# Two v loads on Sync's queue, two casts on Scalar, and block 1's turning one unit later

## The chip, the cores and the metric

The kernel runs on one core of a Trainium2 chip. A core has five engines with queues of their own: TensorE (PE in the profile; PEld is its weight load), VectorE (DVE), ScalarE (ACT), GpSimd (POOL) and SyncE (SP). Transfers are issued by SP, ACT or POOL and are moved by 16 DMA engines. The metric is the device time of one execution in microseconds. The profile is one execution; its times are counted from the start of its span.

## The reference, cut to what matters

Linear attention with a decay per head, followed by a gated feed-forward layer. There are 4 batches, 8 heads, 768 positions and a head size of 64; the layer has a width of 512 and a hidden width of 1536.

```python
for b in range(nb):                     # blocks of the sequence
    intra = einsum('bhic,bhjc->bhij', qb, kb) * Dmask[None]
    intra = einsum('bhij,bhjd->bhid', intra, vb)
    inter = einsum('bhid,bhde->bhie', qb * lam_pow[None], kv_state)
    out[:, :, sl] = intra + inter
    kv_state = lam_block * kv_state + einsum('bhsd,bhse->bhde', kb * rev_pow, vb)
x = out.transpose(0, 2, 1, 3).reshape(B * S, H * D)
gate = 1 / (1 + exp(-(x @ w_gate)))
return (gate * (x @ w_val)) @ w_out
```

All inputs and the output are fp32 in memory. Dmask is lam to the power of the distance, and zero above the diagonal.

## The kernel before

The sequence is cut into six blocks of 128 positions. A block holds 4 x 128 = 512 tokens, all batches together. Matmuls take bf16 and sum in fp32. For each block the kernel does three things. It computes the attention: q and k are transposed, multiplied (`sp`), multiplied by the decay mask (`MT`), multiplied by v (`op`), and the result is cast into `XT`, the transposed input of the layer. It computes 12 units of the hidden layer: for each 128 hidden columns a gate matmul with WG, a sigmoid (`sg`), a value matmul with WV, and a product (`ht`). And it multiplies the 12 `ht` tiles by WO for each batch (`po`), copies the result to `ob` and stores it. The state `Sb` is carried from block to block.

The order of work on each engine is the program's own order: the kernel is written with a manual schedule, in which each engine runs its instructions as the Python code issues them. Waits between engines are put in by the framework.

These parts touch the change:

- **The loads of block 0** (lines 112 to 152). q of batch 0 comes as fp32 into `q01[0]` over ACT's queue, q of batch 1 into `q01[1]` over SP's. VectorE casts the first (line 500) and ACT the second (line 165) into `Q[0]`. All other loads are issued by POOL, with a cast to bf16 on the way, in this order: k of batches 0 and 1, k of 2 and 3, q of 2, q of 3, v of 0, v of 1, v of 2, then the first 128 columns of WG, v of 3, the first 128 columns of WV, and the next 128 columns of each. WG and WV in chunks of 256 columns follow.
- **The small constants** (lines 154 to 173). ACT makes `lnl`, `pk`, `lnp`, `lamq0`, the cast of q of batch 1, `kds` and `dec`. `lamq0` scales the transposed q of block 0. The mask is made by VectorE from `tri` and `pk` in two halves (`make_mask`).
- **Attention of block 0** (lines 499 to 534). `piece_tq0` transposes and scales one batch's q. `piece_tk0` transposes two batches' k; its copies to `KS` are ACT's, but for one on VectorE. `piece_s` multiplies, `piece_m` masks, `piece_a0` multiplies by v and casts to `XT[0]`, on ACT but for the last half. ACT loads the table for the sigmoid (line 512) after the second pair's `KS` copies. `idle(n)` issues n matmuls on a tile of zeros, which feed nothing. The first hidden unit is written out in parts between the last steps.
- **Weights and block 1's inputs** (lines 536 to 543). POOL issues chunk 3 of WG and WV, makes `KD[0]`, then loads q and k of block 1's first two batches, chunk 4, chunk 5, and the rest of block 1. Chunk i holds hidden units 2i and 2i + 1.
- **The units of block 0, and the attention of block 1's first pair between them** (lines 565 to 590). `t(1, 0)` transposes q and k of block 1's first two batches on PE, `sc` multiplies and masks the first, `m` masks the second, and `a` multiplies by state and v and casts to `XT[1]`, two copies on ACT (line 340). They stand between units 7 and 11.
- **The stores** (line 493). SP issues them. For block 0 the tiles of batches 0 and 1 are stored in two halves of 64 rows.

Of the kernel before, what the change touches and what calls it, by code (L numbers as in the profile page):

```python
# [7 lines left out]
FP32 = mybir.dt.float32  # L8
BF16 = mybir.dt.bfloat16
AF = mybir.ActivationFunctionType  # L10
# [5 lines left out]
def kernel(  # L16
# [11 lines left out]
    nc = tc.nc  # L28

    B, H, S, D = q.shape  # L30
    C = 128
# [38 lines left out]
    def load(n, what, b0, b1):  # L70
        sl = slice(n * C, (n + 1) * C)
        for c in what:
            lst, src = {"q": (Q, q), "k": (K, k), "v": (V, v)}[c]
            if n > 1 and c != "v":
                lst[n] = qkv.tile([128, 2, B, HP, D], BF16, tag=c + "b", name=c + "b")
                for e in range(2):
                    nc.gpsimd.dma_start(  # L77
                        out=lst[n][:, e].rearrange("p b y d -> p (b y) d"),
                        in_=src[:, e::2, sl, :].rearrange("b y s d -> s (b y) d"))
                continue  # L80
            if n == 1 and c != "v":
                if n not in lst:
                    lst[n] = qkv.tile([128, 2, B * H * D // 2], BF16, tag=c + "b", name=c + "b")
                if b0 == 0:
                    nc.gpsimd.dma_start(
                        out=lst[n][:, 0].rearrange("p (x d) -> p x d", d=D),
                        in_=src[b0:b1, :, sl, :].rearrange("b h s d -> s (b h) d"))
                else:
                    for e in range(2):
                        nc.gpsimd.dma_start(  # L90
                            out=lst[n][:, 1].rearrange("p (e x d) -> p e x d", e=2, d=D)[:, e],
                            in_=src[b0:b1, e::2, sl, :].rearrange("b y s d -> s (b y) d"))
                continue
            if n not in lst:
                lst[n] = qkv.tile([128, B, H, D], BF16, tag=c + "b", name=c + "b")
            nc.gpsimd.dma_start(  # L96
                out=lst[n][:, b0:b1],
                in_=src[b0:b1, :, sl, :].rearrange("b h s d -> s (b h) d"))
# [5 lines left out]
    def load_gv(i, w):  # L104
        load_w(WG, wg_r, i, w)
        load_w(WV, wv_r, i, w)
# [5 lines left out]
    q01 = [const.tile([128, H, D], FP32, tag=f"q{b}f", name=f"q{b}f") for b in range(2)]  # L112
    nc.scalar.dma_start(out=q01[0], in_=q[0, :, 0:C, :].rearrange("h s d -> s h d"))
    nc.sync.dma_start(out=q01[1], in_=q[1, :, 0:C, :].rearrange("h s d -> s h d"))
    Q[0] = qkv.tile([128, B, H, D], BF16, tag="qb", name="qb")
    nc.scalar.preload_act_table_set("natural_log_exp_and_others")
    ident = const.tile([128, 128], BF16, tag="ident")
# [23 lines left out]
    load(0, "k", 2, 4)  # L141
    load(0, "q", 2, 3)
    load(0, "q", 3, 4)
    load(0, "v", 0, 1)
    load(0, "v", 1, 2)
    load(0, "v", 2, 3)
    GW = DFF // 6
    load_w(WG, wg_r, 0, GW // 2)
# [4 lines left out]

    lnl = const.tile([128, H], FP32, tag="lnl")
    nc.scalar.activation(lnl, lam_bc, AF.Ln)
    pk = const.tile([128, H], FP32, tag="pk")
    nc.scalar.activation(pk, lnl, AF.Exp, scale=jn[:, 0:1])
    lnp = const.tile([128, HP], FP32, tag="lnp")
    for u in range(2):
        us = slice(u * 64, (u + 1) * 64)  # L160
# [1 line left out]
    lamq0 = const.tile([128, HP, C], BF16, tag="lamq0")  # L162
    for hp in range(HP):
        nc.scalar.activation(lamq0[:, hp, :], ip1, AF.Exp, scale=lnp[:, hp:hp + 1])
    nc.scalar.copy(Q[0][:, 1], q01[1])
    kds = const.tile([128, H], FP32, tag="kds")
    nc.scalar.activation(kds, lnl, AF.Exp, scale=jn[:, 1:2])
# [22 lines left out]
    def make_mask(u):  # L190
        nc.vector.tensor_tensor(
            out=mask[:, u::2, :], in0=tri.unsqueeze(1).to_broadcast([128, HP, C]),
            in1=pk[:, u::2].unsqueeze(2).to_broadcast([128, HP, C]), op=ALU.mult)
# [21 lines left out]
    def idle(n):  # L215
        for i in range(n):
            nc.tensor.matmul(wm, lhsT=zero[:, :128], rhs=zero, start=True, stop=True,
                             skip_group_check=True)
# [33 lines left out]
    def piece_tq0(bs, then=None):  # L252
        tq = ps_at.tile([128, 2, 2, 2 * C], BF16, name="tq", tag="ps")
        for b in bs:
            if (0, b // 2) not in QS:
                QS[0, b // 2] = trsb.tile([128, 2, 2, 2, C], BF16, tag="QS", name="QS")
            for g in range(HP):
                transpose_pair(tq[:, b % 2, g // 2, g % 2 * C:g % 2 * C + C], Q[0], b, g)
        if then:
            then()  # L260
        for b in bs:
            nc.vector.tensor_tensor(out=QS[0, b // 2][:, :, b % 2].rearrange("p e x c -> p e (x c)"),
                                    in0=tq[:, b % 2], in1=lamq0_e, op=ALU.mult)

    def piece_tk0(bp):
        tk = ps_at.tile([128, 2, 2, 2 * C], BF16, name="tk", tag="ps")
        for i in range(2):
            for g in range(HP):
                transpose_pair(tk[:, i, g // 2, g % 2 * C:g % 2 * C + C], K[0], 2 * bp + i, g)
        KS[0, bp] = trsb.tile([128, 2, 2, 2, C], BF16, tag="KS", name="KS")  # L270
        for i in range(2):
            cp = nc.vector.tensor_copy if bp == 0 and i == 0 else nc.scalar.copy
            cp(KS[0, bp][:, :, i].rearrange("p e x c -> p e (x c)"), tk[:, i])
# [44 lines left out]
    def piece_a(n, pairs):  # L318
        OP = {(bp, u): ps_at.tile([128, 2, 2, C], FP32, name="op", tag="ps")
              for bp in pairs for u in range(2)}  # L320
        for bp in pairs:
            for i in range(2):
                for x in range(2):
                    for u in range(2):
                        for e in range(2):
                            nc.tensor.matmul(OP[bp, u][half(e), x, i, :],  # L326
                                             lhsT=Sb[half(u), 2 * bp + i, 2 * e + x, :],
                                             rhs=QS[n, bp][half(u), e, i, x, :],
                                             start=(i == 0 and x == 0), stop=False,
                                             skip_group_check=True)  # L330
        for bp in pairs:
            for u in range(2):
                for i in range(2):
                    for x in range(2):
                        intra(n, 2 * bp + i, OP[bp, u][:, x, i, :], 2 * x + u, False, i == 1 and x == 1)
        if n not in XT:
            XT[n] = xtp.tile([128, NMT, B, C], BF16, tag="XT", name="XT")
        for bp in pairs:
            for u in range(2):
                nc.scalar.copy(XT[n][:, u::2, 2 * bp:2 * bp + 2, :], OP[bp, u])  # L340

    def piece_a0(b, split=False):
        if 0 not in XT:
# [89 lines left out]
    def mm_part(ps, W, n, ft, lo, hi):  # L433
        x = XT[n].rearrange("p m b c -> p m (b c)")
        for mt in range(NMT):
            nc.tensor.matmul(ps[:, lo:hi], lhsT=W[:, mt, ft * 128:(ft + 1) * 128], rhs=x[:, mt, lo:hi],  # L436
                             start=(mt == 0), stop=(mt == NMT - 1))

    def psum():
        return ps_ff.tile([128, TCH], FP32, name="gp", tag="ff")  # L440

    def sigm(n, ft, gp):
        HT[n, ft] = htp.tile([128, TCH], BF16, tag="sg", name="sg", bufs=3)
        nc.scalar.activation(HT[n, ft], gp, AF.Sigmoid)
# [37 lines left out]
    def piece_po(n, tt):  # L482
        po = ps_ff.tile([128, DM], FP32, name="po", tag="ff")
        for ft in range(NFT):
            nc.tensor.matmul(po, lhsT=HT[n, ft][:, tt * 128:(tt + 1) * 128],  # L485
                             rhs=WO[:, ft, :], start=(ft == 0), stop=(ft == NFT - 1))
        ob = osb.tile([128, DM], FP32, tag="ob", name="ob")
        nc.scalar.copy(ob, po)  # L488
        parts = 2 if n == 0 and tt < 2 else 1
        rows = 128 // parts  # L490
        for i in range(parts):
            lo = tt * S + n * C + i * rows
            nc.sync.dma_start(out=out[lo:lo + rows, :], in_=ob[i * rows:(i + 1) * rows, :])


    load_gv(1, GW)
# [1 line left out]

    idle(10)
    nc.vector.tensor_copy(Q[0][:, 0], q01[0])  # L500
    piece_tq0([0], lambda: make_mask(0))
    make_mask(1)
    idle(1)
    piece_tq0([1])
    piece_tk0(0)
    idle(1)
    piece_s(0, [0])
    piece_m(0, 0)
# [26 lines left out]

    load_gv(3, GW)
    make_kd(0)
    load(1, "qk", 0, 2)
    load_gv(4, GW)
    load_gv(5, GW)  # L540
    load(1, "v", 0, 2)
    load(1, "qk", 2, 4)
# [1 line left out]
    def t(n, bp):  # L544
        piece_t(n, bp)
# [8 lines left out]
    def a(n, *pairs):  # L554
        piece_a(n, pairs)

    def gv(n, *fts):
        for ft in fts:
            piece_gv(n, ft)
# [20 lines left out]
    for i in range(3):  # L580
        load_wo(i, NFT // 3)
    gv(0, 5, 6, 7)
    t(1, 0)
    gv(0, 8)
    sc(1, 0)
    gv(0, 9)
    m(1, 0)
    gv(0, 10)
    a(1, 0)
    gv(0, 11)  # L590
    transpose_half()
    load(2, "qkv", 0, B)
    transpose_by_dma(2)
# [91 lines left out]
```

## Time and profile before

| | |
|---|---|
| time, median of 3 runs | 227.29 us (227.24 to 228.84) |
| profiled execution | 227.16 us, span 225.4 us |
| granted TensorE clock | 1.000 |
| PE busy | 218.3 us (97%) |
| DVE busy | 103.2 us (46%) |
| POOL busy | 80.9 us (36%) |
| ACT busy | 79.8 us (35%) |
| queue q0 (POOL's transfers) | 81232 packets, 13.90 MB |
| queue q1 (SP's transfers) | 23568 packets, 11.28 MB |

A row of a group or timeline gives the start, the time taken, the engine and line, the operation, output <- input, and in square brackets the idle time before it and what ended it. Rows of matmuls overlap at their ends by the pipeline's depth. A DMA's "landing" is the time from its issue to the semaphore that says it is complete. The share of a queue is the sum of its packets' times over the time of all 16 engines, so several queues, or one with several packets under way in an engine, can exceed 100%.

### The profile page before, as it was taken

The numbers are of one execution on the slowest core, as the hardware profiler recorded it, in microseconds if no ns is written. First come the engines' busy times: TensorE is split into PE (matmuls) and PEld (weight loads), VectorE is DVE, ScalarE is ACT, GpSimd is POOL, SyncE is SP. The second block draws the span as 40 slices with busy tenths as digits, with TensorE's granted clock in tenths as the row PEclk, the third lists the DMA queues.
The fourth block names the chain that finished last, engine by engine and source line by source line (L and its number), as shares of the span: only waits on it lengthen the run. The fifth ranks groups of instructions, "written<-read, shape, count | busy, mean of one in ns | idle before, by whom it ended". The sixth has DMA issues, their size and how long they took to land.

```text
span 225.4 us, 4297 instructions
## 1 busy us (share of the span) xinstructions
PE 218.3 (97%) x1766; PEld 114.4 (51%) x1766; DVE 103.2 (46%) x190; ACT 79.8 (35%) x150; POOL 80.9 (36%) x76
## 2 busy tenths in 40 slices
PE   7689999999999999999999999999999999999994
PEld 2443454888854455444545444446444445444443
DVE  7865737486431622435742345742334850333300
ACT  3664243434422225333215333225333224433221
POOL 8999967983691007940005950000000000000000
DMA  6999999999999992999021999321900012100022
GB/s 109 156 173 195 173 193 156 155 198 166 157 172 181 208 188 82 208 154 119 2 96 47 183 155 157 20 96 50 225 9 0 0 49 93 49 0 0 0 93 97
DMA packets 105860, 25.72 MB, mean 114 GB/s; under 512 B 95984, under 2 KB 102896, under 8 KB 105840
## 3 DMA queue, kind: packets, MB, share of 16 engines
q0 software_dynamic: 81232, 13.90, 80.8%
q1 hardware_dynamic: 23568, 11.28, 20.5%
q10 hardware_dynamic: 1040, 0.26, 0.5%
q8 instruction: 14, 0.23, 0.5%
q14 instruction: 6, 0.05, 0.1%
HBM read 28.32 MB, written 6.29 MB: 154 GB/s over the span
## 4 chain that ended last, share of the span: by engine, by line
PE 91%; POOL 4%; DMA 3%; issue 0%; DVE 0%; POOLq 0%
PE po L485 27%; PE vp L428 22%; PE gp L422 22%; PE gp L457 5%; PE vp L463 5%; DMA WV<-in_moe_w_val_dram 3%; PE sp L302 2%; PE op L314 2%; PE gp L436 2%; POOL vb L96 2%; PE op L326 1%; PE cp L406 1%; PE po L474 1%; POOL kb L96 1%; POOL qb L96 1%; POOL WG L102 1%
## 5 line engine op out<-in xcount | busy, mean ns | idle before, releaser
L431 DVE TENSOR_TENSOR ht<-sg,vp 128x512 bf16<-128x512 bf16 x57 | 39.2, 688 | 68.5 <-PE vp L428 68.5
L485 PE MATMUL po<-WO,ht 128*128 128x512 bf16 x276 | 61.9, 379 | 0.0
L428 PE MATMUL vp<-XT,WV 128*128 128x512 bf16 x228 | 58.5, 379 | 0.4 <-DMA WV<-in_moe_w_val_dram 0.4
L422 PE MATMUL gp<-XT,WG 128*128 128x512 bf16 x228 | 58.6, 379 | 0.0
L425 ACT ACTIVATE sg<-gp 128x512 bf16<-128x512 f32 x57 | 34.1, 598 | 62.3 <-PE gp L422 62.2
L485 PEld LDWEIGHTS <-ht 128*128 128x128 bf16 x276 | 26.3, 98 | 31.0
L428 PEld LDWEIGHTS <-WV 128*128 128x128 bf16 x228 | 22.2, 98 | 27.6 <-DMA WV<-in_moe_w_val_dram 0.9
L422 PEld LDWEIGHTS <-WG 128*128 128x128 bf16 x228 | 21.7, 98 | 25.7
L488 ACT COPY ob<-po 128x512 f32<-128x512 f32 x23 | 13.5, 587 | 52.2 <-PE po L485 50.4
L199 DVE TENSOR_TENSOR MT<-sp,mask 128x512 bf16<-128x512 f32 x40 | 25.2, 683 | 10.0 <-PE sp L302 10.0
L387 POOL TENSOR_TENSOR sd<-Sb,dec 128x512 f32<-128x512 bf16 x8 | 8.2, 1037 | 43.2 <-DVE Sb L413 43.2
L457 PE MATMUL gp<-XT,WG 128*128 128x256 bf16 x96 | 14.4, 273 | 0.0
L463 PE MATMUL vp<-XT,WV 128*128 128x256 bf16 x96 | 14.4, 273 | 0.0
L467 DVE TENSOR_TENSOR ht<-sg,vp 128x256 bf16<-128x256 bf16 x24 | 10.0, 420 | 8.6 <-PE vp L463 8.6
L460 ACT ACTIVATE sg<-gp 128x256 bf16<-128x256 f32 x24 | 9.2, 385 | 12.6 <-PE gp L457 11.5
L96 POOL DMA_DIRECT2D vb<-in_v_dram x10 | 12.8, 1280 | 1.0 <-DVE QS L248 0.8
L378 POOL TENSOR_TENSOR kd<-kb,kds 128x1024 bf16<-128x1024 bf16 x6 | 11.3, 1906 | 3.5 <-DMA kb<-in_k_dram 3.5
L413 DVE TENSOR_TENSOR Sb<-cp,sd 128x512 bf16<-128x512 f32 x8 | 5.2, 686 | 15.5 <-PE cp L406 15.5
L340 ACT CAST XT<-op 128x512 bf16<-128x512 f32 x20 | 10.4, 599 | 3.0 <-PE op L314 3.0
L457 PEld LDWEIGHTS <-WG 128*128 128x128 bf16 x96 | 9.2, 98 | 1.7 <-issue 0.4
L463 PEld LDWEIGHTS <-WV 128*128 128x128 bf16 x96 | 9.4, 98 | 1.1
L77 POOL DMA_DIRECT2D qb<-in_q_dram x8 | 9.4, 1181 | 0.0
(82 smaller groups left out, 148.7 us busy)
## 6 DMA issues: line engine op xcount, KB each, us to landing
out_dram<-ob SPq DMA_DIRECT2D x21, 256.0 KB, 2.1
kb<-in_k_dram POOLq DMA_DIRECT2D x11, 256.0 KB, 8.8
qb<-in_q_dram POOLq DMA_DIRECT2D x9, 256.0 KB, 8.0
vb<-in_v_dram POOLq DMA_DIRECT2D x4, 512.0 KB, 14.1
WO<-in_moe_w_out_dram POOLq DMA_DIRECT2D x3, 512.0 KB, 8.2
WG<-in_moe_w_gate_dram POOLq DMA_DIRECT2D x5, 256.0 KB, 8.6
WV<-in_moe_w_val_dram POOLq DMA_DIRECT2D x5, 256.0 KB, 9.2
qb<-in_q_dram POOLq DMA_DIRECT2D x4, 128.0 KB, 8.1
```

What stands on the lines that cost most here:

```text
L96: nc.gpsimd.dma_start(out=lst[n][:, b0:b1], in_=src[b0:b1, :, sl, :].rearrange("b h s d -> s (b h) d"))
L199: nc.vector.tensor_tensor(out=out.rearrange("p (e x) c -> p e x c", e=2), in0=x.rearrange("p (e x) c -> p e x c", e=2), in1=mask.rearrange ...
L340: nc.scalar.copy(XT[n][:, u::2, 2 * bp:2 * bp + 2, :], OP[bp, u])
L378: nc.gpsimd.tensor_tensor(out=KD[n][:, e], in0=K[n][:, e], in1=kds[:, e::2].unsqueeze(1).unsqueeze(3).to_broadcast([128, B, HP, D]), op=AL ...
L422: nc.tensor.matmul(gp, lhsT=WG[:, mt, fs], rhs=x[:, mt, :], start=(mt == 0), stop=(mt == NMT - 1))
L425: nc.scalar.activation(sg, gp, AF.Sigmoid)
L428: nc.tensor.matmul(vp, lhsT=WV[:, mt, fs], rhs=x[:, mt, :], start=(mt == 0), stop=(mt == NMT - 1))
L431: nc.vector.tensor_mul(HT[n, ft], sg, vp)
L457: nc.tensor.matmul(gp[:, cs], lhsT=WG[:, mt, fs], rhs=x[:, mt, cs], start=(mt == 0), stop=(mt == NMT - 1))
L463: nc.tensor.matmul(vp[:, cs], lhsT=WV[:, mt, fs], rhs=x[:, mt, cs], start=(mt == 0), stop=(mt == NMT - 1))
L485: nc.tensor.matmul(po, lhsT=HT[n, ft][:, tt * 128:(tt + 1) * 128], rhs=WO[:, ft, :], start=(ft == 0), stop=(ft == NFT - 1))
L488: nc.scalar.copy(ob, po)
```

## The change

Five edits in one.

- v of batches 0 and 1 of block 0 is no longer loaded by POOL. SP loads it as fp32 into `q01[0]` and `q01[1]` once the q in them has been cast, and ACT casts it into `V[0]`, behind its first `KS` copy of block 0.
- ACT makes `pk` after `lamq0`. VectorE makes the first half of the mask after the first scaled q, and the second after the first pair's `KS`.
- Chunk 4 of WG and WV, units 8 and 9, is loaded ahead of block 1's first q and k; `t(1, 0)` comes after unit 8, `sc` and `m` after unit 9.
- Unit 11 is written in two parts with `a(1, 0)` between gate and value. Of that call's two `XT` copies one is VectorE's.
- The first two output tiles are stored whole.

```diff
+    V[0] = qkv.tile([128, B, H, D], BF16, tag="vb", name="vb")
...
-    load(0, "v", 0, 1)
-    load(0, "v", 1, 2)
     load(0, "v", 2, 3)
...
-    pk = const.tile([128, H], FP32, tag="pk")
-    nc.scalar.activation(pk, lnl, AF.Exp, scale=jn[:, 0:1])
...
     for hp in range(HP):
         nc.scalar.activation(lamq0[:, hp, :], ip1, AF.Exp, scale=lnp[:, hp:hp + 1])
+    pk = const.tile([128, H], FP32, tag="pk")
+    nc.scalar.activation(pk, lnl, AF.Exp, scale=jn[:, 0:1])
     nc.scalar.copy(Q[0][:, 1], q01[1])
...
-                nc.scalar.copy(XT[n][:, u::2, 2 * bp:2 * bp + 2, :], OP[bp, u])
+                cp = nc.vector.tensor_copy if n == 1 and bp == 0 and u else nc.scalar.copy
+                cp(XT[n][:, u::2, 2 * bp:2 * bp + 2, :], OP[bp, u])
...
-        parts = 2 if n == 0 and tt < 2 else 1
-        rows = 128 // parts
-        for i in range(parts):
-            lo = tt * S + n * C + i * rows
-            nc.sync.dma_start(out=out[lo:lo + rows, :], in_=ob[i * rows:(i + 1) * rows, :])
+        nc.sync.dma_start(out=out[tt * S + n * C:tt * S + (n + 1) * C, :], in_=ob)
...
     nc.vector.tensor_copy(Q[0][:, 0], q01[0])
-    piece_tq0([0], lambda: make_mask(0))
-    make_mask(1)
+    for b in range(2):
+        nc.sync.dma_start(out=q01[b], in_=v[b, :, 0:C, :].rearrange("h s d -> s h d"))
+    piece_tq0([0])
+    make_mask(0)
     idle(1)
     piece_tq0([1])
     piece_tk0(0)
+    make_mask(1)
+    for b in range(2):
+        nc.scalar.copy(V[0][:, b], q01[b])
     idle(1)
...
     load_gv(3, GW)
     make_kd(0)
+    load_gv(4, GW)
     load(1, "qk", 0, 2)
-    load_gv(4, GW)
     load_gv(5, GW)
...
     gv(0, 5, 6, 7)
+    gv(0, 8)
     t(1, 0)
-    gv(0, 8)
+    gv(0, 9)
     sc(1, 0)
-    gv(0, 9)
     m(1, 0)
     gv(0, 10)
+    g11 = psum()
+    mm_part(g11, WG, 0, 11, 0, TCH)
+    sigm(0, 11, g11)
     a(1, 0)
-    gv(0, 11)
+    v11 = psum()
+    mm_part(v11, WV, 0, 11, 0, TCH)
+    prod(0, 11, v11)
```

## The prediction

> **What bounds the kernel now.** First the list of cores, for the clock (granted 1.000) and the span, then the page's chain that ended last.
>
> ```profile
> span 225.4 us, 4297 instructions
> ...
> PE 91%; POOL 4%; DMA 3%; issue 0%; DVE 0%; POOLq 0%
> ```
>
> TensorE (PE) sets the end. The chain in order of time shows from where on:
>
> ```profile
> 11.19 7.30 DMA WV<-in_moe_w_val_dram
> 18.53 1.04 PE vp L428 x4
> 19.57 3.53 PE gp L436 x16
> ```
>
> Until 18.48 the chain runs through GpSimd's DMA issues and the transfer of WV's columns 128 to 255. From 18.53 to the last po at 222.55 PE follows PE with no hole of importance. So a change that does no arithmetic less can only move the point at which PE becomes gapless: every us that the second unit's value matmul (18.53) moves, the end moves, unless a new hole opens later. Outside the span lie 1.76 us (profiled execution 227.16, span 225.4); this one is 0.13 under the median of 227.29.
>
> What PE needs before 18.53 is XT of block 0, which Scalar (ACT) makes. Its timeline:
>
> ```profile
> 8.70 0.59 ACT L273 COPY KS<-tk 128x512 bf16<-128x512 bf16 x1 [0.88 <-DVE KS L273]
> 10.33 1.07 ACT L273 COPY KS<-tk 128x512 bf16<-128x512 bf16 x2 [1.04 <-PE tk L244]
> 11.42 1.28 ACT L512 ACT_TABLE_LOAD   x1
> 13.14 1.69 ACT L353 CAST XT<-op 128x512 bf16<-128x512 f32 x3 [0.44 <-PE op L314]
> ```
>
> The third XT cast ends at 14.83; PE's row for the first unit (L436) starts at 14.88. From there PE works without a hole through L422 at 17.07, four matmuls at 0.22 each, so it is ready for 18.53's matmul at about 17.98. ACT's row has 18.53 - 17.98 = 0.55 us of slack, and no more.
>
> The DMA view of 6 to 10 us, of 4 to 6 us, and of 62 to 64 us (packets, MB, share of 16 engines):
>
> ```profile
> q0 software_dynamic: 4918, 0.62, 244.2%
> ```
> ```profile
> q0 software_dynamic: 1122, 0.14, 112.1%
> q1 hardware_dynamic: 917, 0.23, 51.1%
> ```
> ```profile
> q1 hardware_dynamic: 828, 0.21, 80.1%
> q0 software_dynamic: 826, 0.11, 80.0%
> ```
>
> GpSimd's queue q0 is full when the new loads would run: 4918 / 4 = 1230 packets per us, between 147 and 160 GB/s in every fortieth of the window. A head's row is one packet, so one batch of q, k or v is 128 x 8 = 1024. Sync's packet takes 0.511 x 2 x 16 / 917 = 17.8 ns of an engine.
>
> Last, Sync's rows for an output tile of 256 KB: one issued at 72.3 while q0 was full, and nine from 123.4 on, when it mostly was not; then the transpose issued at 56.04, also under a full q0:
>
> ```profile
> L493 SPq DMA_DIRECT2D out_dram<-ob x1: 375/375/375, 72.3 to 72.3; - x1
> ...
> DMA to landing us min/median/max: 5.7/5.7/5.7
> ```
> ```profile
> L493 SPq DMA_DIRECT2D out_dram<-ob x9: 332/332/333, 123.4 to 192.1; - x9
> ...
> DMA to landing us min/median/max: 2.0/2.0/3.0
> ```
> ```profile
> L235 SPq DMA_TRANSPOSE QR<-qb x1: 4874/4874/4874, 56.0 to 56.0; - x1
> ...
> DMA to landing us min/median/max: 10.9/10.9/10.9
> ```
>
> A transfer of Sync that comes behind a full q0 lands about 3.6 us later (5.7 against 2.1, the page's median). This decides the case.
>
> **What the Trainium skill says.** "DMA: Bandwidth & Descriptors", section "Issuing engines are not separate DMA queues": transfers of all issuers run on the same 16 engines and interleave. The trace agrees: 828 against 826 packets above. The same page, "Queues, rings and completion order", has each engine go round its queues packet by packet; that alone would not hold back a transfer by 3.6 us, so here the measurement decides. "TensorE: Matmul & The Clock Gate", section "Architectural detail: the array is 16× 32×32, not 1× 128×128": ACT's queue is strictly first in, first out; ACT's rows come in program order here. The same page, "What's actually happening": after an idle window of some 3.4 us PE drops to half clock. No wait of PE before is that long; its first ten matmuls take 4.45 us together, 0.44 each against 0.22 later, which fits a cold start.
>
> **The change, part by part.**
>
> *Two v loads leave GpSimd.* Each issue row is 0.88 us, so every later issue comes up to 1.76 us earlier. But q0 is full of data, not short of issues, and the 2 x 1024 packets still pass the same engines. In q0 they took 2048 / 1230 = 1.67 us. Bounds for the weights' landing: 1.67 earlier, if Sync's packets cost the stream nothing; 2048 x 17.8 ns / 16 = 2.28 us of engine time instead of 1.67, so 0.6 later. I take zero. A gain needs XT earlier too, beyond 0.55 us.
>
> *The loads on Sync.* v0 overwrites q01[0], free when the DVE cast L500 ends (4.94 + 0.78 = 5.72): issue at 5.75. v1 waits for ACT's cast of q01[1]. With pk behind lamq0, ACT no longer waits 0.82 us for jn: lnp starts at 4.04, lamq0 ends near 5.75, pk near 6.0, the cast runs 6.0 to 6.6 (q1f landed at 1.21 + 4.7 = 5.91): issue at 6.65. At 5.75 four block 0 loads of q0 have been issued (k twice, two q; 6144 packets), of which no more than 1122 have run by 6 us, so v0 meets the full queue. Its landing: the like transfer q0f took 4.2 from issue, some 1 us of it from sharing with q1f; 3.2 to 4.2, plus 3.6: v0 lands at 12.55 to 13.55. v1 follows in the same queue: its 1024 packets add 1024 x 17.8 / 16 = 1.14 us if Sync has the engines alone, 1024 / 414 = 2.47 at the even split of 62 to 64 us. So v1 lands between 13.7 and 16.0. I take 14.4, nearer the low end, since Sync's plain copies are shorter per packet (17.8 ns) than the transposes of that split (0.801 x 2 x 16 / 828 = 31 ns). Without the 3.6 us it would be 10.1 to 12.4.
>
> *The casts on ACT.* They stand between KS of b0, i=1 (L273, done about 8.8) and the two KS copies of the second pair. Queued behind them: both KS copies, the table load L512, the four XT casts. Behind KS waits PE with piece_s(0,[2]), behind that DVE with MT. From v1's landing: one cast 0.60 (row L165), KS 1.07, table load 1.28, three XT casts 1.69, some 0.1 of handovers: 4.75. (PE's and DVE's part, s(2), MT, s(3), a0, is done inside that, by about 3.75 after the landing, and v2 and v3 are then long there.) First unit at 14.4 + 4.75 = 19.15 instead of 14.88: 4.27 late. Less the slack of 0.55: **3.7 us later**. The weights that paced PE (WV at 18.48, the next WG at 11.92 + 7.5 = 19.4) have then landed, so nothing is late behind it and nothing is won back. General form: delay = landing of v1 - 10.7.
>
> *Idle PE.* q3's transposes end at about 11.1; then PE waits for KS until 15.6. 4.5 us exceed the skill's window. If the clock falls, up to 3.4 us of work run at half speed, 1.7 us lost; if the window falls badly, nothing. Not in my value, in the range.
>
> *mask and pk.* Same instructions, other order. DVE loses its 0.51 us wait for lamq0, but ends at the wait for KS. Zero; if v were early, its cover is ACT's slack, worth at most 0.5.
>
> *Unit 8's weights first, block 1 turned one unit later.* WG and WV of chunk 4 took slots behind q and k; they landed at 22.7 + 8.1 = 30.8 and 23.5 + 8.6 = 32.1, for use at 31.68 and 32.55. Now two slots earlier, and q and k two later: k from 29.4 to about 32.1, against turning at 32.4 plus the delay of PE. All four hidden; if k were 1 us late, 0.7 us of PE. Zero.
>
> *Unit 11 in two parts, one XT copy on DVE.* Before, XT of the first pair was copied by ACT (1.07, L340) under gate and value of unit 11 (1.83). Now it has only the value's 0.86 above it, but two copies on two engines, 0.6 each. DVE has unit 10's product and four MT in front (5 x 0.62 from about 35.9, ready at 39.0 where a(1,0) ends near 39.3). Bounds 0 to 0.3; I take zero.
>
> *Two output tiles unsplit.* Two issues of about 0.5 us less on Sync, far behind PE. Zero.
>
> Sum: 227.16 + 3.7 = 230.9.
>
> **Rivals.** (1) *Sync's loads are not held back* (q0 backs off, as q0 did from 4.3 to 5 us when q1f was first in line). v1 lands at 10.2 to 11.5; delay 0 to 0.8: 227.2 to 228.0. Speaks for it: that early stretch. Against: there the hardware queue was first; behind a full q0 all rows are late. (2) *Half of it*: landing 11.5 to 13.4, delay 0.8 to 2.7: 228.0 to 229.5. (3) *Not slower: the weights come earlier.* If the two v's run in gaps of q0, WV and the next WG land up to 1.67 us earlier; with v1 in by 10.2, XT keeps its pace or gains the 0.5 us of pk, and PE becomes gapless 0.2 to 1.4 us sooner: 225.8 to 227.0. It decides only if v1 lands before 10.7. Against: 1230 packets per us without a dip.
>
> **How the numbers follow.** Forecast 0.63 (landing 13.4 to 16, delay 2.7 to 5.3, own range 229.6 to 232.4, above that with a fallen clock), rival 1 0.19, rival 2 0.09, rival 3 0.09. Range 227.3 to 232.4: it leaves out rival 3 (0.09), 0.03 of rival 1 and some 0.07 of the forecast, mostly with the half clock. 1% of 227.29 is 2.27 us, about what a measurement of this kernel can tell from no change: slower (over 229.56) takes nearly all of the forecast, 0.62; faster (under 225.02) only the end of rival 3, 0.02; the rest 0.36.
>
> **What would show it.** Right: v's rows on Sync with a landing of 7 us or more; ACT's first wait for v0, then the KS pair near 15 instead of 10.33; XT near 19; no DMA as releaser of L428; a hole of PE of 4 us before the third batch's L302. Wrong: landings under 5 us, or the chain still through WV's transfer. Equal times after 24 us would show the other parts at zero.

## The result, and the profile after

| | before | after |
|---|---|---|
| time, median of 6 runs each | 227.22 us (227.12 to 228.84) | 233.94 us (233.43 to 234.48) |
| profiled execution | 227.16 us, span 225.4 | 234.48 us, span 232.7 |
| granted TensorE clock | 1.000 | 0.985 |
| second unit's value matmul (L428) starts | 18.53 us | 24.94 us |
| last po's group (L474) starts | 219.92 us | 226.44 us |

The line of an operation moves by a few from kernel to kernel: the second unit's value matmul is L428 in these two, and L427 to L431 in others.

The changed kernel is slower by 6.7 us: the ratio of the times is 1.028, with a 95% interval from 1.025 to 1.032. The direction and the place were forecast. The size was not: 233.94 lies above the range, which ended at 232.4.

The page of the kernel after: the slices with the granted clock, and the shares of the chain.

```profile
PEclk9985999999999999999999999999999999999999
...
PE 90%; DMA 6%; issue 1%; ACT 1%; SPq 0%; DVE 0%
```

PE still sets the end. The fourth slice of the clock (17.5 to 23.3 us) is new: 5 instead of 9, half speed for most of it. DMA's share of the chain has risen from 3% to 6%, and the transfer in it is another. Here is the chain in order of time (start, duration, what):

```profile
6.66 9.07 DMA q1f<-in_v_dram
15.73 0.02 issue
15.76 0.62 ACT vb L506
16.38 0.49 ACT KS L272
...
16.91 1.09 PE sp L301 x12
...
21.50 1.19 PE gp L436 x4
```

Before, the chain ran through WV's weights until 18.48. Now it runs through v of batch 1: issued at 6.66, landed 9.07 us later, cast on ACT, and only then the KS copies that PE waits for. ACT's timeline shows what stands in the queue behind that wait:

```profile
12.79 0.62 ACT L506 CAST vb<-q0f 128x512 bf16<-128x512 f32 x1 [3.74 <-DMA q0f<-in_v_dram]
15.76 0.62 ACT L506 CAST vb<-q1f 128x512 bf16<-128x512 f32 x1 [2.35 <-DMA q1f<-in_v_dram]
16.28 1.06 ACT L272 COPY KS<-tk 128x512 bf16<-128x512 bf16 x2
17.36 1.28 ACT L513 ACT_TABLE_LOAD   x1
18.66 1.07 ACT L353 CAST XT<-op 128x512 bf16<-128x512 f32 x2
20.58 0.59 ACT L353 CAST XT<-op 128x512 bf16<-128x512 f32 x1 [0.85 <-PE op L313]
```

The KS pair has gone from 10.33 to 16.28 and the third XT cast from an end of 14.83 to 21.17. ACT waits 6.09 us for the two v's, and in the last line 0.85 us for PE, a wait that the prediction's sum did not have. PE's timeline says why:

```profile
16.91 1.09 PE L301 MATMUL sp<-QS,KS 64*128 64x128 bf16 x16 [4.76 <-ACT KS L272]
...
21.30 1.40 PE L436 MATMUL gp<-XT,WG 128*128 128x384 bf16 x4
...
24.94 1.03 PE L428 MATMUL vp<-XT,WV 128*128 128x512 bf16 x4
```

PE stands idle for 4.76 us; then sixteen products take 1.09 (0.73 before), and L436 takes 1.40 (0.81 before). The windows view gives the granted clock for each 2 us (stage, length, then busy time and number of instructions of PE, PEld, DVE, ACT and POOL, then clock, DMA share and GB/s):

```profile
14.00:16.00 2.00, 0.00 (x0) 0.00 (x0) 0.00 (x0) 0.24 (x1) 0.82 (x2) 0.91 1.91 164
16.00:18.00 2.00, 1.09 (x18) 0.75 (x20) 0.44 (x1) 1.98 (x4) 1.94 (x3) 0.50 1.78 180
...
20.00:22.00 2.00, 1.67 (x12) 0.94 (x14) 0.04 (x1) 0.59 (x1) 2.00 (x3) 0.50 1.45 200
22.00:24.00 2.00, 2.00 (x22) 1.11 (x21) 0.42 (x1) 0.37 (x1) 2.00 (x4) 0.88 1.46 194
```

The clock is 0.50 from 16 to 22 us, just when everything that waited is to be made up for. In windows of a tenth of a microsecond it falls at 15.65 and is full again at 22.48.

From 24.94 on the two kernels run almost alike: L428 is 6.41 us late, and PE's last group 6.52 us late, so only 0.11 us more is lost in the 195 us between. The profiled execution is 0.8 us longer than that (7.32 against 6.52). That rest lies behind PE's end, in the last two output stores on Sync. Here they are before and after:

```profile
222.41 0.82 SPq L480 DMA_DIRECT2D out_dram<-ob  x2
```
```profile
228.94 1.19 SPq L480 DMA_DIRECT2D out_dram<-ob  x2
```

The second store is issued 0.37 us later behind the first, and lands in 2.0 us instead of 1.6. Why is open. The profiled execution is the longest of the six, so how the 6.7 us between the medians divide between PE and these stores is not known.

The time up to L428 decomposes as follows. v1 landed at 15.73. The prediction's ACT chain of 4.75 would then bring the first unit at 20.48; it started at 21.30, 0.82 later, because ACT's third XT cast waited for a half-speed PE. From L436 to L428 took 3.64 instead of the 3.10 that the prediction had for a full clock: 0.54. So half clock has 1.36 us in this trace, by arithmetic on the prediction's figures. A kernel below measures it: 1.6.

### The profile page after: what moved, and what is told of

It reads as the page before. It is cut to its first block, busy times and chain, and to the rows that moved or that the text cites. A ratio compares the mean times of both kernels' runs of the same rounds, so it can differ in the third digit from the quotient of the medians.

```text
span 232.7 us, 4274 instructions
## 1 busy us (share of the span) xinstructions
PE 219.1 (94%) x1742; PEld 115.3 (50%) x1766; DVE 103.9 (45%) x191; ACT 80.3 (35%) x151; POOL 79.1 (34%) x74
## 4 chain that ended last, share of the span: by engine, by line
PE 90%; DMA 6%; issue 1%; ACT 1%; SPq 0%; DVE 0%
PE po L485 26%; PE gp L422 21%; PE vp L428 21%; PE gp L457 5%; PE vp L463 5%; DMA q1f<-in_v_dram 4%; PE gp L436 3%; PE op L313 3%; PE sp L301 3%; DMA q1f<-in_q_dram 2%; PE op L325 1%; PE cp L406 1%; PE po L474 1%; PE wm L216 1%; ACT vb L506 0%
## 5 line engine op out<-in xcount | busy, mean ns | idle before, releaser
L431 DVE TENSOR_TENSOR ht<-sg,vp 128x512 bf16<-128x512 bf16 x56 | 38.5, 687 | 66.3 <-PE vp L428 62.1
L422 PE MATMUL gp<-XT,WG 128*128 128x512 bf16 x217 | 57.0, 379 | 0.5
L428 PE MATMUL vp<-XT,WV 128*128 128x512 bf16 x220 | 56.6, 379 | 0.1
L425 ACT ACTIVATE sg<-gp 128x512 bf16<-128x512 f32 x56 | 33.4, 597 | 62.5 <-PE gp L422 61.3
L428 PEld LDWEIGHTS <-WV 128*128 128x128 bf16 x224 | 21.9, 98 | 26.7 <-issue 0.3
L457 PE MATMUL gp<-XT,WG 128*128 128x256 bf16 x96 | 14.4, 273 | 0.0
L463 PE MATMUL vp<-XT,WV 128*128 128x256 bf16 x96 | 14.4, 273 | 0.0
L96 POOL DMA_DIRECT2D vb<-in_v_dram x8 | 11.1, 1383 | 1.1 <-DMA kb<-in_k_dram 1.1
L340 ACT CAST XT<-op 128x512 bf16<-128x512 f32 x19 | 9.9, 598 | 2.1 <-PE op L313 2.0
```

The lines of the kernel that those rows point to most:

```text
L96: nc.gpsimd.dma_start(out=lst[n][:, b0:b1], in_=src[b0:b1, :, sl, :].rearrange("b h s d -> s (b h) d"))
L422: nc.tensor.matmul(gp, lhsT=WG[:, mt, fs], rhs=x[:, mt, :], start=(mt == 0), stop=(mt == NMT - 1))
L425: nc.scalar.activation(sg, gp, AF.Sigmoid)
L428: nc.tensor.matmul(vp, lhsT=WV[:, mt, fs], rhs=x[:, mt, :], start=(mt == 0), stop=(mt == NMT - 1))
L431: nc.vector.tensor_mul(HT[n, ft], sg, vp)
L457: nc.tensor.matmul(gp[:, cs], lhsT=WG[:, mt, fs], rhs=x[:, mt, cs], start=(mt == 0), stop=(mt == NMT - 1))
```

## Experiments

**Is it the v's alone?** The first theory is the prediction's: two v's that land late and hold ACT. The rival is that one of the other four edits takes a part of the 6.7 us. The first kernel keeps those edits and gives v back to GpSimd; the second puts the v's alone into the kernel before.

```diff
+    load(0, "v", 0, 1)
+    load(0, "v", 1, 2)
     load(0, "v", 2, 3)
...
-    for b in range(2):
-        nc.sync.dma_start(out=q01[b], in_=v[b, :, 0:C, :].rearrange("h s d -> s h d"))
...
-    for b in range(2):
-        nc.scalar.copy(V[0][:, b], q01[b])
```

> The whole change except its v part: both v's are loaded by POOL again, with no cast on ACT; the constants' order, unit 8's weights, block 1's turning, unit 11's split and the whole stores stay as changed. Theory (v1's landing behind a full q0 is the cause, the other parts cost nothing): 226.7 to 227.7, no difference from before that can be told, PE at full clock, and the second unit's value matmul at 18.0 to 18.6. Rival (part of the 6.7 us comes from the new order of block 1 and of unit 11, or from the mask): 228.5 or more, with a hole of PE between 30 and 47 us.

The second kernel is the kernel before with the reverse of this diff.

> The kernel before with the v part alone: v of batches 0 and 1 on SP's queue into the q tiles, the two casts on ACT at the same place. Theory: 233.4 to 234.5; v1 lands at 15.5 to 16.0, since it follows v0 in Sync's queue whether it is issued at 6.7 or at 7.4; clock under 1. Rival (the parts work together): 230 to 232.5.

Measured: 227.58 us without the v part, against 227.34 for the kernel before (ratio 1.0009, 1.0003 to 1.0016), and 233.79 with the v part alone (1.028, 1.026 to 1.031), where v1 landed at 15.7. Both are inside their forecasts. Without the v part PE waits for WV again, by the chain and by PE's timeline:

```profile
11.18 7.57 DMA WV<-in_moe_w_val_dram
```
```profile
18.79 1.04 PE L430 MATMUL vp<-XT,WV 128*128 128x512 bf16 x4 [0.86 <-DMA WV<-in_moe_w_val_dram]
```

The start at 18.79 is just above the expected 18.0 to 18.6, since WV's transfer took 7.57 us instead of 7.30. The v part is the whole loss but for the 0.2 us that the other four edits cost together; and as these are already there at 18.79, the new order of block 1 and of unit 11 costs nothing that shows. The rival falls.

**How much is the half clock?** Twenty matmuls on zeros in PE's wait keep it busy. They add nothing to the result. The theory that the clock costs 1.4 us expects most of that back.

```diff
     piece_tq0([3])
+    idle(20)
```

> The changed kernel with 20 more matmuls on the tile of zeros between the last q transposes and the third batch's scores; they take up 4.3 of the 4.8 us in which PE waits, and feed nothing. Theory (1.36 of the 6.5 us are PE's clock at half rate after that wait): granted clock 1.000, time 1.1 to 1.6 us under the changed kernel's, so 232.3 to 232.9; v1 lands at 15.7 as before. Rival (the half clock lies under ACT's casts and costs nothing): 233.6 to 234.3.

Measured: 233.48 us (233.42 to 233.53, ratio 1.027, 1.025 to 1.029), 0.5 better than after instead of 1.1 to 1.6: a miss. The clock was full (0.996 to 1.0), and L428 started at 23.31, 1.63 earlier than after. So the clock's part was there, and then it was lost again. PE's timeline of this kernel:

```profile
20.25 0.81 PE L436 MATMUL gp<-XT,WG 128*128 128x384 bf16 x4 [0.49 <-ACT XT L353]
...
23.31 1.03 PE L428 MATMUL vp<-XT,WV 128*128 128x512 bf16 x4
...
29.39 1.02 PE L428 MATMUL vp<-XT,WV 128*128 128x512 bf16 x4 [0.73 <-DVE ht L449]
```

v1 landed at 15.71 here, and the first unit came 4.54 us later: at full clock ACT's chain takes 4.54, not 4.75. The last row shows a hole of 0.73 us, where after lost 0.1 and the kernel before nothing. VectorE's timeline shows what it does before that `ht`:

```profile
25.05 0.98 DVE L180 COPY lp<-lam_bc 64x4 f32<-64x4 f32 x2
26.06 1.85 DVE L184 TENSOR_TENSOR lp<-lp 128x4 f32<-128x4 f32 x7
27.95 0.80 DVE L187 CAST lamq<-lp 128x512 bf16<-128x512 f32 x1
28.67 1.27 DVE L449 TENSOR_TENSOR ht<-sg,gp 128x512 bf16<-128x512 bf16 x2
```

`make_lamq`, the table of decay powers for later blocks, stands in VectorE's order right behind the second unit's product, ahead of the next two. It takes 3.6 us, and PE has hardly more work than that to go on with. Two kernels, made from the fed one, move it: behind the products of units 2 and 3, or into VectorE's own wait in front of MT.

```diff
     idle(20)
...
     gv(0, 1)
-    make_lamq()
...
         prod(0, ft, vp)
+    make_lamq()
     gv(0, 4)
```

> The kernel of the fed PE (20 more matmuls on zeros in its wait) with make_lamq behind the products of units 2 and 3 instead of ahead of them, so that VectorE doesn't hold back these products. Theory (a full clock is worth 1.6 us at the second unit's value matmul, of which 0.7 is lost again to VectorE's lamq at the fifth unit's value matmul): the hole of 0.73 us there is gone, PE ends another 0.7 us earlier, time 232.5 to 233.0. Rival (the time comes back through another wait): 233.3 to 233.6.

Measured: 233.86 us. The forecast of 232.5 to 233.0 missed, and the rival's 233.3 to 233.6 too. The hole had moved, and grown from 0.73 to 1.26 us:

```profile
32.34 1.02 PE L428 MATMUL vp<-XT,WV 128*128 128x512 bf16 x4 [1.26 <-DVE ht L431]
```

Earlier, then:

```diff
     idle(20)
+    make_lamq()
...
     gv(0, 1)
-    make_lamq()
```

> The kernel of the fed PE (20 more matmuls on zeros in its wait) with make_lamq in VectorE's own wait, ahead of the third batch's scores, instead of behind the second unit. Theory (a full clock is worth 1.5 us, and reaches the end only if VectorE isn't late right behind it): no hole of PE at the fifth unit, clock 1.000, time 232.1 to 232.7, that is 0.8 to 1.4 under the fed kernel's 233.48. Rival (another wait takes the hole's place, as with lamq later): 233.3 to 233.9.

And the same move without the matmuls on zeros, so that the pair differs in the clock alone:

> The changed kernel with make_lamq in VectorE's wait alone, PE not fed. Theory: with the half clock PE comes so late that VectorE's lamq held it back by only 0.1 us; time 233.2 to 234.4 as the changed kernel's, clock 0.985. Rival (lamq is itself what costs the time): 232.1 to 232.9.

Measured: 232.73 us with the zeros (232.70 to 232.84, clock 1.000) and 233.89 without (233.67 to 234.32, clock 0.985). The first is 0.03 over the upper edge of its forecast, the second inside. In the first the hole is gone:

```profile
23.29 1.03 PE L428 MATMUL vp<-XT,WV 128*128 128x512 bf16 x4
...
28.47 1.03 PE L428 MATMUL vp<-XT,WV 128*128 128x512 bf16 x4
```

The difference of 1.16 us is what a full clock is worth in this change once VectorE is out of the way, in the medians. In single traces it depends on when the clock falls. Half clock lasted 6.8 us in after, in the kernel with early `make_lamq` and in the one with the v part alone, but it began at 15.65, 14.96 and 13.39. PE's rows of the last two:

```profile
24.57 1.03 PE L428 MATMUL vp<-XT,WV 128*128 128x512 bf16 x4
```
```profile
24.16 1.03 PE L427 MATMUL vp<-XT,WV 128*128 128x512 bf16 x4
```

So the second unit's value matmul came at 24.94, 24.57 and 24.16, against 23.29 with the zeros: 1.65, 1.28 and 0.87 us. This may be why the executions of after spread from 233.43 to 234.48; the others have no trace.

Of what is left at a full clock, 232.73 - 227.34 = 5.4 us, 4.7 are waiting for v: L428 is 4.76 late there, and PE ends 4.68 late. The rest lies behind PE's end again.

**Does the loss follow the landing?** The prediction's general form was: delay = landing of the last v - 10.7. With v of batch 0 alone on Sync, and one cast, the landing should be v0's.

```diff
+    load(0, "v", 1, 2)
     load(0, "v", 2, 3)
...
-    for b in range(2):
-        nc.sync.dma_start(out=q01[b], in_=v[b, :, 0:C, :].rearrange("h s d -> s h d"))
+    nc.sync.dma_start(out=q01[0], in_=v[0, :, 0:C, :].rearrange("h s d -> s h d"))
...
-    for b in range(2):
-        nc.scalar.copy(V[0][:, b], q01[b])
+    nc.scalar.copy(V[0][:, 0], q01[0])
```

> The changed kernel with v of batch 0 alone on SP's queue, with one cast; v of batch 1 is loaded by POOL again. Theory (delay = landing of the last v on Sync's queue - 10.7, as predicted[...]): the v lands near 12.7, PE's wait for KS is under 2.5 us and its clock stays 1.000, delay 2.0, time 229.0 to 229.8. Rival (each cast and load costs a fixed amount, half of the whole): 230.3 to 230.8.

ACT's timeline of this kernel:

```profile
12.81 0.62 ACT L505 CAST vb<-q0f 128x512 bf16<-128x512 f32 x1 [3.71 <-DMA q0f<-in_v_dram]
```

v0 landed at 12.8, so the form gives 12.8 - 10.7 = 2.1 us. The profiled execution, at full clock, was 229.52, 2.2 over the median of the kernel before; PE ended 2.17 later. That the two numbers agree is in part luck, as PE's timeline shows:

```profile
17.33 0.81 PE L437 MATMUL gp<-XT,WG 128*128 128x384 bf16 x4 [0.49 <-ACT XT L354]
...
20.39 1.03 PE L429 MATMUL vp<-XT,WV 128*128 128x512 bf16 x4
...
25.98 1.02 PE L429 MATMUL vp<-XT,WV 128*128 128x512 bf16 x4 [0.25 <-DVE ht L450]
```

The second unit's value matmul is only 1.86 late (20.39 against 18.53), since ACT's chain took 4.5 us here too; the hole behind `make_lamq` brings most of the rest. The median was 230.22 (ratio 1.013, 1.010 to 1.016), above the forecast of 229.0 to 229.8, because two of the four executions ended at 230.9 and 231.1. Their mean clock was 0.993 and 0.992, where the forecast had 1.000. For these two there is no trace, so it stays open where in them the clock fell, and that it costs them the 1.5 us is argued only.

**Why does v land so late?** The theory: it stands behind the transfers that GpSimd issued before it. The rival: Sync's fp32 loads take 7 to 9 us by themselves, or because the two queues share the engines. The DMA view of after from 5.5 to 9.5 us has one row (queue, packets, MB, share of 16 engines):

```profile
q0 software_dynamic: 4918, 0.62, 244.4%
```

Sync's queue, q1, moved nothing from 5.5 until 9.6, 3.8 us after v0's issue. By then GpSimd's had moved 5584 of the 6144 packets that were issued before v0. If GpSimd pauses before its second load, there is less in front. Four small products on GpSimd make the pause:

```diff
+    pad = const.tile([128, TCH], BF16, tag="pad")
+    for i in range(4):
+        nc.gpsimd.tensor_tensor(out=pad, in0=zero, in1=zero, op=ALU.mult)
     load(0, "k", 2, 4)
```

> The changed kernel with four small products on GpSimd, some 4 us together and read by nobody, between its first and its second load of k: so Sync's v0, issued at 5.8, finds only one load of k ahead of it, which is nearly through. Looked at for the landing of the two v's; the time will be longer, since k and q of the later batches come 4 us later. Theory (a transfer is served in the order of arrival behind what is already queued[...]): v0 lands 3 to 4.5 us after its issue instead of 7.0, v1 by 4.5 us instead of 9.1. Rival (Sync's copies in rows of 256 bytes are always this slow beside GpSimd's queue): 6.5 us or more for v0.

The issue on Sync of v0 in this kernel (ns per issue, when, then the time from issue to landing as min/median/max):

```profile
L501 SPq DMA_DIRECT2D q0f<-in_v_dram x1: 378/378/378, 7.5 to 7.5; - x1
...
DMA to landing us min/median/max: 3.1/3.1/3.1
```

The DMA view from 8.5 to 10 us shows v0's packets almost alone:

```profile
q1 hardware_dynamic: 1000, 0.25, 73.8%
q0 software_dynamic: 109, 0.01, 14.5%
```

With the engines not yet full, v0 landed 3.1 us after its issue; in after it took 7.0. v1, issued at 8.01, took 6.9: from 10 to 11.5 us GpSimd's queue moved 1599 packets, of the k load that it had issued from 7.03 to 8.27, and Sync's 100. The forecast of 4.5 or less for v1 missed, because the pause was over. So a load of this kind isn't slow by itself: the transfer whose packets came ahead of k's took 3.1, the one whose packets came behind them 6.9. The time (232.89 us, one execution) was no better, because GpSimd's loads behind the pause were late. The chain runs through q now:

```profile
8.27 6.97 DMA qb<-in_q_dram
```

That can be pushed further. If order of issue decides, v should land early when it is issued right after q, in tiles of its own, ahead of most of GpSimd's loads:

```diff
+    v01 = [const.tile([128, H, D], FP32, tag=f"v{b}f", name=f"v{b}f") for b in range(2)]
+    for b in range(2):
+        nc.sync.dma_start(out=v01[b], in_=v[b, :, 0:C, :].rearrange("h s d -> s h d"))
...
-    for b in range(2):
-        nc.sync.dma_start(out=q01[b], in_=v[b, :, 0:C, :].rearrange("h s d -> s h d"))
...
-        nc.scalar.copy(V[0][:, b], q01[b])
+        nc.scalar.copy(V[0][:, b], v01[b])
```

> The changed kernel with two fp32 tiles of their own for v of batches 0 and 1, so that Sync issues both loads right behind q of batch 1, near 1.6 and 2.0 us, before GpSimd's queue has moved anything; the casts stay where they are. Theory (Sync's transfers are late because they come behind a full q0): from issue to landing 4.5 to 6 us instead of 7.0 and 9.1, v1 in by 8; ACT doesn't wait for it; instead k of the first batches lands some 2 us later, since Sync is now first, and delays the first unit by 1 to 2 us; clock 1.000; time 227.7 to 229.2. Rival (fp32 rows of 256 bytes and two casts on ACT are slow by themselves): 231 or more.

Measured: 232.4 us (ratio 1.022, 1.019 to 1.025), a clear miss, and a number that the rival had (231 or more). Sync's timeline of this kernel:

```profile
1.66 0.58 SPq L117 DMA_DIRECT2D v0f<-in_v_dram  x1
2.28 3.18 SPq L117 DMA_DIRECT2D v1f<-in_v_dram  x1
```

And PE's timeline of it:

```profile
9.36 0.62 PE L246 MATMUL tk<-ident,kb 128*128 128x128 bf16 x8 [1.57 <-DMA kb<-in_k_dram]
...
12.89 1.04 PE L246 MATMUL tk<-ident,kb 128*128 128x128 bf16 x8 [1.16 <-DMA kb<-in_k_dram]
```

v0 landed at 8.2, but v1 only at 12.9, and now k is late: the first k landed 8.1 us after its issue instead of 6.0, the second 10.3 instead of 6.4. The order works in both directions. A transfer that goes in front pushes back what stood there, and k is needed before v. PE waited at k's transposes instead, and its clock was at half from 10.6 to 17.4 us.

The start of the issue doesn't decide the order, though: v1's began at 2.28, ahead of GpSimd's second k load (2.54), and v1 still landed 10.6 us later. Its issue lasted until 5.46. Some 180 packets of Sync's queue moved from 6.6 to 7.2 us, then only 15 until 9.0, while GpSimd's moved 2188. What held v1's packets back is open.

**How much is ACT's order?** The KS copies and the table load need no v. Here the casts stand behind them, each ahead of the product that reads it:

```diff
     piece_tk0(0)
     make_mask(1)
-    for b in range(2):
-        nc.scalar.copy(V[0][:, b], q01[b])
...
+    nc.scalar.copy(V[0][:, 0], q01[0])
     piece_a0(0)
+    nc.scalar.copy(V[0][:, 1], q01[1])
     piece_a0(1)
```

> The changed kernel with ACT's two casts moved behind the second pair's KS copies and the table load, one ahead of each of the first two products with v; the loads are the same. Theory (what is queued behind the casts on ACT makes the landing cost so much): v0 and v1 land at 12.7 and 15.7 as before, KS and the table load are done by 12.6, behind v1's cast stand only three XT casts and a product, the first unit starts near 18.1, clock 1.000, time 229.4 to 230.4. Rival (the landing alone decides, wherever the casts stand): 233 or more.

Measured: 233.1 us (ratio 1.025, 1.023 to 1.027): again a miss, by 2.7 us, and the rival's number (233 or more, wherever the casts stand). But the trace shows that the order has its worth. KS stood at 10.15 and the table was loaded by 12.5, as planned. The first unit came at 19.32, 2.0 us earlier than in after. PE's timeline shows where the rest went:

```profile
16.39 0.64 PE L313 MATMUL op<-MT,vb 128*64 128x128 bf16 x8 [2.51 <-ACT vb L522]
...
29.42 1.02 PE L428 MATMUL vp<-XT,WV 128*128 128x512 bf16 x4 [0.71 <-DVE ht L449]
```

v1's landing still holds PE, the products behind it ran at half clock (0.64 for eight, where 0.41 is usual), and `make_lamq` cut its hole of 0.7 us here too, so that PE ended only 0.9 us earlier than in after. To see the order's worth without the clock, eleven matmuls on zeros fill this wait:

```diff
     nc.scalar.copy(V[0][:, 1], q01[1])
+    idle(11)
     piece_a0(1)
```

> The kernel with ACT's casts behind the KS copies and the table load, with 11 more matmuls on zeros between the first and the second product with v, in PE's wait of 2.5 us. Theory (with ACT's queue and the half clock out of the way, what is left is v1's landing): clock 1.000, the first unit starts at 17.9 to 18.6 instead of 19.3, the second unit's value matmul at 21.1 to 21.8 instead of 23.4, and up to 0.9 us are lost behind it to VectorE's lamq: time 230.0 to 231.4. Rival (the waits on ACT and PE's clock are not what holds it): 232.5 or more.

Measured: a median of 230.87 us (ratio 1.015, 1.013 to 1.016), inside its forecast. Four of six executions took 230.78 to 230.91 at a clock of 0.997 to 1.000, two 232.34 and 232.40 at 0.993. The profiled one is of the latter. In it the zeros themselves ran at half clock (11 in 4.00 us) and held PE until 17.97, so the first unit came at 19.95, and the 17.9 to 18.6 of the forecast has no trace that shows it. A full clock and ACT's order together are thus worth some 3 us of the 6.7, in the medians. How the remaining 3.5 us divide between v1's landing, `make_lamq`'s hole and the stores behind PE's end is not shown. No version was faster than the kernel before.

## Why the prediction was wrong, by its steps

- **Where PE becomes gapless sets the end**: held. L428 moved by 6.41 us and the last po by 6.52.
- **The casts on ACT, 4.75 from v1's landing, slack 0.55**: held in kind, and 0.2 us too long. At full clock the chain took 4.5 us, with both v's and zeros as with one v. So the form gives some 0.25 too much (with one v 2.1 against 1.86 at the second unit's value matmul), which `make_lamq`'s hole hid in the end time.
- **The loads on Sync**: the first failed step. The mechanism was right: v0 landed at 12.74, inside 12.55 to 13.55, and with no backlog it took 3.1 us instead of 7.0. The size of v1's term was off. "I take 14.4, nearer the low end, since Sync's plain copies are shorter per packet (17.8 ns) than the transposes of that split" is where it fell: it measured 15.73, 1.33 more. The DMA view of after, from 10.5 to 12.5 us, has the even split that this sentence set aside:

```profile
q1 hardware_dynamic: 837, 0.21, 80.2%
q0 software_dynamic: 835, 0.11, 80.1%
```

  As many packets of one queue as of the other, whatever their length, as in the transposes' row, and 837 in 2 us is 418 per us, just the 414 on which 2.47 us for v1 rested. With the even split the working gave 15.0 to 16.0. Even that was a little short: v1 landed 2.99 us after v0 instead of 2.47, and from 12 to 14 us the two queues moved only 770 and 771 packets. The argument from the packet's length had no row behind it; the row against it was in the text.
- **Idle PE**: the second failed step. "Not in my value, in the range" gave zero to a cost whose mechanism was stated (from the Trainium skill, "TensorE: Matmul & The Clock Gate", section "What's actually happening") and whose condition, a wait of 4.5 us, the sum itself had produced. It measured 1.65 us in the trace of after, and 1.16 in the medians of the pair with and without zeros. Nor did the range hold it: its upper edge, 232.4, is the landing at 16.0 (5.3 us) alone. With a fallen clock (1.7) that is 234.2, which contains the 233.94; the fallen clock was left outside as a small chance. It was no small chance: with PE waits of 4.6 to 4.8 us in the traces (after, the v part alone, early `make_lamq` without zeros) all 14 executions had a mean clock of 0.993 or less, with a wait of 1.8 us (one v) two of four. In after the clock fell 3.5 us after PE's last matmul, which agrees with the page's idle window of some 3.4 us. Other traces don't: with the v part alone it fell 1.1 us into the wait, and with the casts behind and zeros it fell when PE had waited at most 1.02 us at a time. So shorter waits can cost the clock too.
- **Two v loads leave GpSimd**: taken as zero; it could not show, since L428 no longer waited for a weight.
- **mask and pk, unit 8's weights, unit 11, the stores**: taken as zero; together 0.2 us, by the kernel that has them all and v on GpSimd.
- **Rivals 1 to 3** (Sync's loads not held back, half of it, the weights earlier): refuted by the landings of 7.0 and 9.1 us.

The sum, with the terms put right: 3.7 + 1.33 for v1's landing, less 0.27 for ACT's shorter chain and a little more slack, is the 4.76 us that L428 was late at full clock; with 1.65 for half clock it is the 6.41 of after's trace. What lies behind PE's end stays open: 0.8 us in the profiled execution of after and some 0.7 in the kernel with zeros and the early `make_lamq`. There are also slips without weight in the prediction's edges: 227.16 plus a delay of 2.7 is 229.9, not 229.5 or 229.6, and plus 5.3 it is 232.5, not 232.4.

## What to carry to other kernels

A transfer on an idle queue is no faster way in where another queue has already filled the DMA engines: price it from a row that was issued behind a full queue, count both transfers at the even split of packets, and look at what else stands behind the wait on the engine that consumes it. Where a sum produces a PE wait longer than any in the profile before, put half clock for what follows into the value, not only into the range; and look at the clock of several executions, since it fell in some of them after shorter waits. When PE is made earlier, look for the next engine whose slack was never tested: here a setup of 3.6 us on VectorE gave back nearly half of two gains (1.63 and 1.57 us at L428, 0.94 and 0.90 at the end); in the first it was moved into VectorE's own wait, and three quarters of a microsecond came back.

## What the runs showed of the hardware that was not expected

- **Mixing the queues costs packets.** Counted from the trace's packets, q0 alone moved 2463 in the 2 us from 6 to 8 us of after, some 616 in half a microsecond; Sync's fp32 loads, all but alone, 1464 in 1.5 us (the kernel with early v, 5 to 6.5 us), some 488; and both together 1672 in 2 us, some 418, half of each. The 209 packets that Sync put in thus took some 407 from GpSimd's queue. If the engines only took turns at the two rates, both together would move some 540 in half a microsecond (an estimate from these two rates). In after, q of batch 3 reached PE a microsecond later (11.76 instead of 10.78), though GpSimd issues it in the same place.
- **An issue on Sync can itself take 3.18 us.** The third batch-sized load in a row did (the timeline of early v above), against 0.37 to 0.58 for the others.
- **VectorE's short copies vary in length.** The two fp32 copies of `lp` took 0.37 together in the kernel before, 0.65 in after and 0.98 in the fed one, the cast of `lamq` 0.43, 0.43 and 0.80, with the same instructions; where they stood early, 0.35 and 0.68. In the kernel with GpSimd's four products VectorE's seven adds at the start took 3.71 us instead of 2.52. The last agrees with the Trainium skill, "SBUF — State Buffer", section "SBUF: two separate sides", by which some operations of VectorE and those of GpSimd exclude each other on a shared pair of ports; that the copies have the same cause is only argued, from GpSimd's DMA issues beside them.
- **The clock can differ between executions of one kernel.** With one v on Sync, or with the casts behind and the wait filled by zeros, executions fell into two groups 1.5 us apart, by 0.992 or 0.993 against 0.997 to 1.000. A low mean alone costs nothing: executions of the kernel before had 0.992 and took 227.30 to 227.42. Where in these the clock fell is not known.
- **Half clock came in pieces of 3.4, 6.8 or 10.2 us.** In the first 25 us it lasted 3.4 with the casts behind and zeros, 6.8 in after and in four other traces, and 10.2 in the kernel with GpSimd's four products.
